# An attention and two dense layers on one core: decays as repeated rows, the causal mask by short products, guards in pairs

## The chip, the cores and the metric

The kernel runs on one core of a Trainium2 chip. Its time is that of one execution on the device in microseconds (us); the runs' median is what two versions are compared by. The engines are called as the profile calls them: PE (matrix products), PEld (its weight loads), DVE (vector), ACT (scalar), POOL (GpSimd) and SP, which issues DMAs; PEq, SPq and so on are an engine's instruction queue.

## The reference

Attention with a decay per head, then a mixture of four experts, then a gated layer. Only the attention is touched by the change:

```python
B, H, S, D = q.shape                      # 2, 8, 576, 64
scores = (1 / np.sqrt(D)) * np.matmul(q, k.transpose(0, 1, 3, 2))
cum = np.cumsum(np.maximum(s, 0.0), axis=-1)
bias = -(cum[:, :, :, None] - cum[:, :, None, :])
scores = np.where(causal, -1e9, scores + np.minimum(bias, 0.0))
attn = np.exp(scores - scores.max(-1, keepdims=True))
attn = attn / (attn.sum(-1, keepdims=True) + 1e-09)
out = np.matmul(attn, v)
...
x = moe(out); return gated(x)             # x: 1152 x 512
```

## The kernel before

Sixteen heads (two batches of eight) are worked two at a time. A *pair* is two heads whose 64 rows of Q and K stand in the two halves of the partitions. The sequence of 576 is cut into blocks of 128 rows (the last has 64). The program first takes the *early* blocks 0 and 1 of all pairs (pairs 0 to 7), then the *late* blocks 2, 3 and 4 (pairs 8 to 15, which are the same heads again). Block 4 has 64 rows, so both heads of a pair share one tile of 128 rows there; this is the two-head block.

For each pair the function `scores` multiplies Q and K in float32 into PSUM (`sp`) and adds the decay on PE: `rk` and `lq` hold the running sums of `s` in two fp32r halves and ones, so that a second product over 64 rows, or 128 for the two-head block, adds cum[key] - cum[query]. The sums are made in `scan` on 16 partitions, split in two halves in `cums` and brought to the rows of `rk` and `rq` by eight DMAs (`rows_of`); `sel` picks a pair's rows when `lq` is scaled. The constant term of a row falls out when the row's minimum is taken off. Then `chain` does, for each head and block of rows: `least` (DVE: adds the causal `mask`, scales, writes `ns` and takes the row's minimum), `exp` (ACT), `guard` (DVE: adds 1e-9 and takes the reciprocal), `norm` (division by the sum, on DVE or POOL), `turn` (PE transposes the blocks of `ns` into `tp`), `copy` (ACT or DVE, into `p`). `products` multiplies by V into `po`, and `values` writes the result in two halves, `xh` and `xl`.

The dense layers read `xh` and `xl`. Weights come by DMA into `raw` and are split into two fp32r halves (`wah` and `wal`, `woh` and `wol`), in the attention stage on POOL. The first dense unit needs the early blocks of four pairs only, so dense products (h and o) stand between the pieces of attention. All instructions are put in order ahead of the run by a planner (`Plan`): every task names its engine or several, its cost, what it depends on, buffers that it takes and gives back, and a rank; the planner starts the earliest task that can go, and where PE would be idle ahead of the first dense output it puts in transposes of the identity (`keep_on`, L426). Engines and DMA queues then work strictly in that order. PSUM holds two score banks `sp`, two `tp`, one `po`, and the dense `h` and `o`.

Of the kernel before, what the change touches and what calls it, by code (L numbers as in the profile page):

```python
# [17 lines left out]
P = 128  # L18
# [8 lines left out]
NL = 3  # L27
# [15 lines left out]
NORM = "pv"  # L43
# [46 lines left out]
def f32(ap):  # L90
    return ap.bitcast(F32)
# [177 lines left out]
def attention_moe_swiglu(ctx, tc, q_early, q_late, k, v, s, dp, w1, w2, wg, wv, wo, out):  # L269
# [23 lines left out]
    wp = ctx.enter_context(tc.tile_pool(name="wp", bufs=2))  # L293
    psw = ctx.enter_context(tc.tile_pool(name="psw", bufs=1, space=PSUM))
# [43 lines left out]
    def attention(ap, ps):  # L338
        one = ap.tile([P, S], F32, name="one", tag="ns", bufs=NS)[:B * H, :]
        sr = ap.tile([P, NB - 1, 320], F32, name="sr", tag="p", bufs=NPT).rearrange("p c t -> p (c t)")[:B * H, :S]  # L340
        ncum = ap.tile([P, S], F32, name="ncum", bufs=1)[:B * H]
        cums = ap.tile([LO + B * H, S], F32R, name="cums", bufs=1)
        cum_at = [slice(0, B * H), slice(LO, LO + B * H)]
# [3 lines left out]
        rk = ap.tile([P, S], F32R, name="rk", bufs=1)  # L347
        rq = ap.tile([P, S], F32, name="rq", bufs=1)
        sel = ap.tile([P, 3, BP], F32, name="sel", bufs=1)

        mask = ap.tile([P, BANK + P], F32, name="mask", bufs=1)
        mask2 = ap.tile([P, D], F32, name="mask2", bufs=1)


        t_sr = add("dma", (0.48, 0.1), lambda: nc.sync.dma_start(sr, s), take=[ring("p", NPT)], rank=-100)
        t_one = any_of("vp", "fill", S - 2 * P, lambda e: {"v": nc.vector, "p": nc.gpsimd}[e].memset(
            one[:, :S - 2 * P], 1.0), [], take=[ring("ns", NS)], rank=-99)
        t_id = add("pool", 0.6, lambda: make_identity(nc, ident), rank=-99)

        def upper():  # L360
            nc.gpsimd.memset(mask[:, BANK:], 0.0)
            nc.gpsimd.affine_select(
                out=mask[:, BANK:], in_=mask[:, BANK:], pattern=[[-1, P]], compare_op=ALU.is_ge, fill=-8.0e30, base=0,
                channel_multiplier=1)
        t_up = add("pool", 0.6, upper, [t_id], rank=-92)
        t_zero = []
        for o, r in ((slice(BANK - P, BANK), -91), (slice(0, BANK - P), 10)):
            t_zero.append(any_of("vp", "fill", o.stop - o.start, lambda e, o=o: {
                "v": nc.vector, "p": nc.gpsimd}[e].memset(mask[:, o], 0.0), [], rank=r))

        def twice(e):
            for x in half:
                move(e, mask2[x, :], mask[x, BANK + x.start:BANK + x.stop])
        t_mask = [t_up, t_zero[0]]
        t_mask2 = [t_up, *t_zero, any_of("vp", "copy", P, twice, [t_up, t_zero[1]], n=2, rank=12)]
# [9 lines left out]
        def rows_of(x, at, deps, rank):  # L385

            t = at
            for i, e in enumerate("vv" if not x.start else "vp"):
                def part(on, i=i):
                    if i:  # L390
                        minus(on, cums[cum_at[1], x], ncum[:, x], cums[cum_at[0], x])
                    else:
                        move(on, cums[cum_at[0], x], ncum[:, x])
                t = any_of(e, "two" if i else "copy", x.stop - x.start, part, [t], rank=rank)
                for j, (to, of) in enumerate(((rk, 2 * i), (rq, 2 * i + 1))):
                    got = fetch(lambda to=to, of=of: f32(to[of::8, x]), f32(cums[cum_at[i], x]), 16, [t] + deps, rank + 0.1 + 0.1 * j)
                    t_rows[x.start].append(got)

        def fetch(to, x, kb, deps, rank, take=(), queue=None):

            return add("dma", (ISSUE, kb * DMA_KB), lambda: (queue or nc.sync).dma_start(to(), x), deps, take=take, rank=rank)

        early, later = slice(0, 2 * P), slice(2 * P, S)
        t_rows = {0: [], 2 * P: []}
        t_fill = [any_of("vp", "fill", 2 * P, lambda e, x=x, y=y: {"v": nc.vector, "p": nc.gpsimd}[e].memset(f32(x[:, early]), y), [], rank=-97)
                  for x, y in ((rk, -1.0), (rq, 1.0))]
# [4 lines left out]
        def pick():  # L411
            nc.vector.reduce_sum(sel[:, 1:].rearrange("p h m -> p (h m)"), ident.rearrange("p (m r) -> p m r", r=8)[:, :, :4], axis=AX.X)
            nc.vector.tensor_tensor(sel[:, 0], sel[:, 1], sel[:, 2], op=ALU.add)
        t_pick = add("dve", 0.35, pick, [t_id], rank=-96)
        t_fill2 = [any_of("p", "fill", S - 2 * P, lambda e, x=x, y=y: nc.gpsimd.memset(f32(x[:, later]), y), [], rank=CUM2)
                   for x, y in ((rk, -1.0), (rq, 1.0))]
        t = any_of("p", "fill", S - 2 * P, lambda e: positive(e, later), [t_sr], rank=CUM2)
        t_scan2 = add("dve", dve(S - 2 * P), lambda: scan(later), [t, t_scan], give=[(t_sr, ring("p")), (t_one, ring("ns"))], rank=CUM2)
        rows_of(later, t_scan2, t_fill2, CUM2)
# [26 lines left out]
        t_ready, t_scores, qs, lq = {}, {}, {}, {}  # L446

        def prepare(pi, release):
# [9 lines left out]
            def to():  # L458
# [5 lines left out]
            parts = [(0, x.start, 0, 2 * P)] if exact else [(0, x.start, 0, 2 * P)] + [  # L464
                (1 + j, 4 * P, 2 * P + j * D, 2 * P + j * D + D) for j in range(2)]
            done = []
            for kind, a, o, e in parts:
                def pick(on, kind=kind, a=a, o=o, e=e):
                    if pi not in lq:
                        lq[pi] = ap.tile([P, n], F32R, name="l" + tag, tag="l" + tag, bufs=NL)  # L470
                    scale(on, lq[pi][:, o:e], rq[:, a:a + e - o], sel[:, kind, m:m + 1])
                done.append(any_of(SPLIT, "scale", e - o, pick, [release, t_pick] + t_rows[x.start][1::2] + done[:1],
                                   take=[] if done else [ring("l" + tag, NL)], rank=rank + 0.2))
            t_ready[pi] = [tk, tq] + done + t_rows[x.start][::2]
            used[pi] = [(tq, ring(tag)), (done[0], ring("l" + tag))]
# [10 lines left out]
        def scores(i, pi, qbs, last):  # L486

            m = pi % BP
            two = rows(qbs[0]) < P
            w = [qb * P + rows(qb) for qb in qbs]  # L490
            box = {"sp": {}}

            def run():
                Q, K, L = qs[pi], keys[m], lq[pi]
                if two:
                    for s0, s1 in ((0, BANK), (BANK, w[0])):
                        sp = ps.tile([P, BANK], F32, name="sp", tag="sp", bufs=2)
                        nc.tensor.matmul(sp[:, :s1 - s0], Q[:, 2 * P:], K[:, s0:s1], start=True, stop=False)  # L498
                        nc.tensor.matmul(sp[:, :s1 - s0], L[:, 2 * P:], rk[:, s0:s1], start=False, stop=True)
                        box["sp"].setdefault((None, qbs[0]), []).append(sp)  # L500
                    return
                sp = [ps.tile([P, BANK], F32, name="sp", tag="sp", bufs=2) for j in range(2)]
                at = 0
                for qb, n in zip(qbs, w):
# [4 lines left out]
                    for j in range(2):  # L509
                        box["sp"][j, qb] = [sp[j][:, at:at + n]]  # L510
                    at += n
            cost = sum(pe32(n) + pe(n) for n in w) + SWITCH
            t = inorder("s", add("pe", cost, run, t_ready[pi] + [before.get("s")], take=[ring("sp")] * 2,
                                 give=used[pi] if last else [], rank=i + RANK["s"]))
            return t, box["sp"]

        def chain(i, pi, ch, j, qb, tS, banks, last_of):

            g = pi // NP
            n = rows(qb)  # L520
            w = qb * P + n
            heads = [j] if j is not None else [0, 1]
            two = len(heads) == 2
            row = {h: slice(x * n, (x + 1) * n) for x, h in enumerate(heads)}
            spans = [(a, min(w, a + BANK)) for a in range(0, w, BANK)]
            box = {}

            def least():
                st = box["st"] = ap.tile([P, 6], F32, name="st", tag="st", bufs=8)
                box["ns"] = ap.tile([P, S], F32, name="ns", tag="ns", bufs=NS)  # L530
                for x, ((s0, s1), sp) in enumerate(zip(spans, banks[j, qb])):
# [1021 lines left out]
```

## Time and profile before

| | |
|---|---|
| median of 3 runs | 721.79 us (721.7 to 722.0) |
| profiled execution: own time, span | 723.54 us, 721.8 us |
| PE busy | 705.4 us, 98% of the span |
| DVE, ACT, POOL busy | 563.6, 350.6, 481.6 us |
| mean granted clock of PE | 0.991 |
| moved by DMA | 71.74 MB, 99 GB/s over the span |

The span runs from the first to the last instruction. PE's busy time is the union of its records, whose ends are modelled, so the distance between starts tells more on the rate of products than their length. A float32 product is two records in the trace and one row in the order of the program; a transpose is one.

### The profile page before, as it was taken

The page shows a single profiled execution, that of the slowest core. Times are in us where ns is not written, and L with a number is a line of the kernel's source. Part 1 is how long each engine was busy: PE and PEld are TensorE (multiplying, and loading weights), DVE is VectorE, ACT ScalarE, POOL GpSimd, SP SyncE. Part 2 cuts the span into 40 slices and gives each one's busy share as a digit, 9 for nine tenths or more (in the row PEclk, how much of TensorE's full clock was granted, in tenths as well). Part 3 has the DMA queues.
Part 4 walks back from the last instruction along what each step waited for, and adds up shares of the span by engine and source line. Part 5 has one row for each costly group of instructions (what it writes and reads, how often), then busy time and mean ns, then how long its engine had stood idle before and what let it go on. Part 6 is the DMA issues. An engine that isn't in the chain of part 4 may idle for free.

```text
span 721.8 us, 11989 instructions
## 1 busy us (share of the span) xinstructions
PE 705.4 (98%) x4256; PEld 609.1 (84%) x4256; DVE 563.6 (78%) x1146; ACT 350.6 (49%) x776; POOL 481.6 (67%) x460
## 2 busy tenths in 40 slices
PE   7899999999999999999999999999999999999997
PEld 6576666688898888898989899998889999999996
DVE  4787767598278799999999897577876878787665
ACT  3687665443434555565565554375654324233210
POOL 3664544699456578765777577699899768585321
PEclk7899999999999999999999999999999999999999
DMA  5362341011304454573455544102011202000003
GB/s 154 136 201 95 115 136 41 30 31 58 117 1 146 163 159 162 178 228 132 147 177 203 190 139 140 58 31 88 30 59 59 63 31 84 30 30 1 1 1 131
DMA packets 26554, 71.74 MB, mean 99 GB/s; under 512 B 3184, under 2 KB 7408, under 8 KB 26496
## 3 DMA queue, kind: packets, MB, share of 16 engines
q1 hardware_dynamic: 26352, 70.86, 29.6%
q8 instruction: 33, 0.54, 0.3%
q14 instruction: 25, 0.20, 0.1%
q10 hardware_dynamic: 144, 0.13, 0.1%
HBM read 59.04 MB, written 11.80 MB: 98 GB/s over the span
## 4 chain that ended last, share of the span: by engine, by line
PE 84%; DVE 9%; issue 2%; POOL 2%; ACT 1%; DMA 1%; SPq 0%; DVEq 0%; POOLq 0%; ACTq 0%
PE o L1120 11%; PE o L1121 11%; PE o L1122 11%; PE h L1058 11%; PE h L1060 11%; PE h L1059 11%; PE sp L508 4%; PE tp L567 3%; PE po L616 3%; PE h L958 2%; PE h L960 2%; PE h L959 2%; DVE tt L997 2%; DVE cc L1077 1%; PE sp L498 1%
## 5 line engine op out<-in xcount | busy, mean ns | idle before, releaser
L1077 DVE TENSOR_TENSOR cc<-cc,h 128x320 f32<-128x320 f32 (+1 forms) x282 | 125.2, 452 | 48.8 <-PE h L1060 43.4
L1120 PE MATMUL o<-woh,hh 128*128 128x512 f32 x396 | 157.6, 398 | 1.6 <-DVE acc_b L1208 0.9
L1121 PE MATMUL o<-wol,hh 128*128 128x512 f32 x396 | 155.9, 394 | 0.0
L1122 PE MATMUL o<-woh,hl 128*128 128x512 f32 x396 | 154.9, 391 | 0.1
L1058 PE MATMUL h<-xh,wsh 128*128 128x320 f32 (+1 forms) x312 | 93.0, 298 | 0.0
L1060 PE MATMUL h<-xh,wsl 128*128 128x320 f32 (+1 forms) x312 | 92.9, 298 | 0.0
L1059 PE MATMUL h<-xl,wsh 128*128 128x320 f32 (+1 forms) x312 | 92.8, 297 | 0.0
L327 POOL TENSOR_TENSOR wal<-raw,wah 128x512 fp32r<-128x512 f32 (+1 forms) x58 | 74.3, 1290 | 27.5 <-ACT wah L314 26.5
L1122 PEld LDWEIGHTS o<-woh,hl 128*128 128x128 f32 x396 | 74.5, 188 | 17.1 <-POOL hl L327 0.6
L1120 PEld LDWEIGHTS o<-woh,hh 128*128 128x128 f32 x396 | 74.6, 188 | 16.0 <-DVE acc_b L1208 1.6
L327 POOL TENSOR_TENSOR hl<-cc,hh 128x512 fp32r<-128x512 f32 (+1 forms) x29 | 43.5, 1500 | 64.8 <-ACT hh L1180 61.5
L327 POOL TENSOR_TENSOR wol<-raw,woh 128x512 fp32r<-128x512 f32 x54 | 78.7, 1470 | 9.4 <-ACT woh L314 8.9
L1121 PEld LDWEIGHTS o<-wol,hh 128*128 128x128 f32 x396 | 74.6, 188 | 10.6
L1177 ACT ACTIVATE cc<-cc 128x640 f32<-128x640 f32 (+1 forms) x46 | 32.0, 696 | 80.8 <-DVE cc L1077 80.8
L1058 PE MATMUL h<-xh,wah 128*128 128x320 f32 (+1 forms) x234 | 69.5, 297 | 0.7 <-DVE cc L1077 0.7
L1060 PE MATMUL h<-xh,wal 128*128 128x320 f32 (+1 forms) x234 | 69.4, 297 | 0.0
L1059 PE MATMUL h<-xl,wah 128*128 128x320 f32 (+1 forms) x234 | 69.4, 296 | 0.0
L327 POOL TENSOR_TENSOR wsl<-sf,wsh 128x512 fp32r<-128x512 f32 x44 | 65.4, 1505 | 0.5 <-ACT wsh L314 0.4
L324 POOL TENSOR_SCALAR ns<-ns,st 128x512 f32<-128x512 f32 (+4 forms) x39 | 22.8, 586 | 60.1 <-DVE st L546 42.9
L1208 DVE SCALAR_TENSOR_TENSOR acc_b<-o,pr,acc_b 128x512 f32<-128x512 f32 x75 | 55.6, 743 | 8.0 <-PE o L1122 7.6
L1058 PEld LDWEIGHTS h<-xh,wsh 128*128 128x128 f32 x312 | 59.0, 189 | 1.5
L1059 PEld LDWEIGHTS h<-xl,wsh 128*128 128x128 f32 x312 | 59.0, 189 | 1.4
(150 smaller groups left out, 1748.8 us busy)
## 6 DMA issues: line engine op xcount, KB each, us to landing
raw<-in_w SPq DMA_DIRECT2D x42, 512.0 KB, 4.5
n<-hl SPq DMA_DIRECT2D x36, 256.0 KB, 2.4
raw<-n SPq DMA_DIRECT2D x18, 512.0 KB, 3.3
hh<-in_wg SPq DMA_DIRECT2D x12, 512.0 KB, 3.8
hh<-in_wv SPq DMA_DIRECT2D x12, 512.0 KB, 4.5
hh<-in_wo SPq DMA_DIRECT2D x12, 512.0 KB, 4.2
vr<-in_v SPq DMA_DIRECT2D x4, 640.0 KB, 4.0
ql<-in_q_late SPq DMA_DIRECT2D x8, 192.0 KB, 3.1
```

What stands on the lines that cost most here:

```text
L324: {"v": nc.vector, "p": nc.gpsimd}[e].tensor_scalar(to, x, by, 1.0, op0=ALU.mult, op1=ALU.mult)
L327: {"v": nc.vector, "p": nc.gpsimd}[e].tensor_tensor(to, x, f32(y), op=ALU.subtract)
L508: nc.tensor.matmul(sp[j][:, at:at + n], y[half[j], x], z[half[j], :n], start=first, stop=not first)
L1058: nc.tensor.matmul(hp, wh, h, start=c == 0, stop=False)
L1059: nc.tensor.matmul(hp, wh, l, start=False, stop=False)
L1060: nc.tensor.matmul(hp, wl, h, start=False, stop=c == 1)
L1077: nc.vector.tensor_tensor(part(k), part(x), banks[i], op=ALU.add)
L1120: nc.tensor.matmul(op, hh[:, f, ts], wh[:, f, :], start=f == 0, stop=False)
L1121: nc.tensor.matmul(op, hh[:, f, ts], wl[:, f, :], start=False, stop=False)
L1122: nc.tensor.matmul(op, hl[:, f, ts], wh[:, f, :], start=False, stop=f == NF - 1)
L1177: nc.scalar.activation(src()[:, o], src()[:, o], AF.Relu)
L1208: nc.vector.scalar_tensor_tensor(acc(t), bank_(), sc, acc(t), op0=ALU.mult, op1=ALU.add)
```

## The change

- The decays are no longer added on PE. `sums` holds the running sum with one column taken off (`center`); it is written to memory, and for each pair a DMA repeats a head's row over the partitions (`dqe` for early pairs, `dql` and, for the two-head block, `d2`). `least` adds these where it added the mask. For pairs 0 and 1 (`NSEL`) PE selects the row by a product with a column of the identity instead, and ACT copies it.
- The causal mask is added on PE: `idr` (identity, 64 rows at a time) times `tri` (0 and -2^103), 128 and 64 columns for each head and block. In the two-head block the mask is added to `d2`'s last 64 columns.
- `scores` and `chain` become `group`. One `guard` serves two rows of sums; the transposes of both early blocks of a head go into one bank and one copy; early score banks of pairs 1 and 3 come from the dense `h` banks.
- `norm` runs on POOL alone (`NORM = "p"`).

```diff
-NL = 3
+NBE = 3
+NBL = 2
+NSEL = 2
...
-NORM = "pv"
+NORM = "p"
...
+        def center(x, at):
+            nc.vector.tensor_scalar(sums[:, x], ncum[:, x], ncum[:, at:at + 1], 1.0, op0=ALU.subtract, op1=ALU.mult)
...
-        rows_of(early, t_scan, t_fill, -97.5)
+        t_early = add("dve", dve(2 * P), lambda: center(early, P - 1), [t_scan], rank=-98)
+        t_rows = [fetch(lambda: rows_e, sums[:, early], 16, [t_early], -97.5)]
...
-                    scale(on, lq[pi][:, o:e], rq[:, a:a + e - o], sel[:, kind, m:m + 1])
...
+            if pi < NSEL:
+                def pick():
+                    bias()
+                    tp = ps.tile([P, BANK], F32, name="tp", tag="tp", bufs=2)
+                    for j in range(2):
+                        nc.tensor.matmul(tp[:, j * w:j * w + w], ident[:BH, BP * j + m:BP * j + m + 1].to_broadcast([BH, P]),
+                                         sums[:, early], start=True, stop=True)
...
+            else:
+                of = rows_e if exact else rows_l
+                first = fetch(bias, lambda: of[m::BP, :w].partition_broadcast(P), 2 * w // 2, [release, t_rows[-1]], rank + 0.2, take=[rg])
...
+                    t2.append(fetch(both(j), lambda j=j: rows_l[BP * j + m, :].partition_broadcast(D), 144, [release, t_rows[-1]] + t2,
+                                    rank + 0.3, take=[] if j else [ring("d2", NBL)]))
...
-                    for y, z, first in ((Q, K, True), (L, rk, False)):
+                    for j in range(2):
+                        nc.tensor.matmul(sp[j][:, at:at + w], Q[half[j], x], K[half[j], :w], start=True, stop=False)
+                    for o, y in enumerate((slice(0, P), slice(P, P + D))):
                         for j in range(2):
-                            nc.tensor.matmul(sp[j][:, at:at + n], y[half[j], x], z[half[j], :n], start=first, stop=not first)
+                            nc.tensor.matmul(sp[j][:, at + w - P + o * D:at + w], idr[half[j], o, :], tri[half[j], y], start=False, stop=o == 1)
...
-                nc.vector.tensor_scalar(st[:, 4:5], st[:, 2:3], 1.0e-9, None, op0=ALU.add)
-                nc.vector.reciprocal(st[:, 5:6], st[:, 4:5])
+                    nc.vector.tensor_scalar(st[:, 12 + x:12 + x + n], st[:, 8 + x:8 + x + n], 1.0e-9, None, op0=ALU.add)
+                    nc.vector.reciprocal(st[:, 16 + x:16 + x + n], st[:, 12 + x:12 + x + n])
```

The planner puts everything in a new order. First PE, from the start of the program to the scores of the first pair (k_104 and the like are a pair's keys, o<-ident the transposes that keep PE moving). Before:

```order
L426 MATMUL o<-ident 128x128 x29
L508 MATMUL sp<-k_104,qe 128x128 x2
L508 MATMUL sp<-rk,lqe 128x128 x2
L508 MATMUL sp<-k_104,qe 128x256 x2
L508 MATMUL sp<-rk,lqe 128x256 x2
L426 MATMUL o<-ident 128x128 x3
```

and after:

```order
L399 MATMUL o<-ident 128x128 x14
L451 MATMUL tp<-sums,ident 128x256 x4
L516 MATMUL sp<-k_106,qe 128x128 x2
L519 MATMUL sp<-tri,idr 128x128 x2
L519 MATMUL sp<-tri,idr 128x64 x2
L516 MATMUL sp<-k_106,qe 128x256 x2
L519 MATMUL sp<-tri,idr 128x128 x2
L519 MATMUL sp<-tri,idr 128x64 x2
L516 MATMUL h<-k_107,qe 128x128 x2
```

The selections of two pairs stand ahead of the first scores, each block's rk products have become four short mask products, and the second pair's scores follow the first's at once, in h banks. Ahead of the first dense product PE has 7 score groups, 34 transposes and 6 value groups before; after, 4 selections, 7 score groups, 30 transposes and 4 value groups. There are 58 transposes of the identity before and 44 after, 10 of them behind the first dense product.

On POOL the place is the early pairs (ns<-ns,st is a division; wah, wal, woh, wol are weights). Before:

```order
L324 TENSOR_SCALAR ns<-ns,st 128x128
L318 TENSOR_SCALAR wah<-raw 128x512
L327 TENSOR_TENSOR wal<-raw,wah 128x512
L324 TENSOR_SCALAR ns<-ns,st 128x256
L318 TENSOR_SCALAR wah<-raw 128x512
L318 TENSOR_SCALAR woh<-raw 128x512
L327 TENSOR_TENSOR wal<-raw,wah 128x512
L327 TENSOR_TENSOR wol<-raw,woh 128x512
```

and after, a little further on:

```order
L327 TENSOR_SCALAR ns<-ns,st 128x128
L327 TENSOR_SCALAR ns<-ns,st 128x256
L321 TENSOR_SCALAR wah<-raw 128x512
L327 TENSOR_SCALAR ns<-ns,st 128x128
L327 TENSOR_SCALAR ns<-ns,st 128x256
L330 TENSOR_TENSOR wal<-raw,wah 128x512
L327 TENSOR_SCALAR ns<-ns,st 128x128
L327 TENSOR_SCALAR ns<-ns,st 128x256
```

Pieces of weights now stand singly between the divisions of each head. On SP, behind the first loads of Q and K, the two pairs of transfers from cums have become one write of the sums and one repeated read. Before:

```order
L401 DMA rk<-cums 16x256 x2
L401 DMA rq<-cums 16x256 x2
L401 DMA k_107<-in_k 128x256
L401 DMA qe<-in_q_early 128x256
L401 DMA vr<-in_v 128x512 x2
```

and after:

```order
L358 DMA rows_104<-sums 16x256
L358 DMA dqe<-rows_104 128x2x256
L358 DMA k_109<-in_k 128x256
L358 DMA qe<-in_q_early 128x256
L358 DMA vr<-in_v 128x512 x2
L358 DMA rows_105<-sums 16x576
```

The keys of the fourth pair and the loads after them stand behind the repeated read of pair 2, as they stood behind the reads of cums.

## Rows read from the trace of the kernel before

**Rows 1.** Stretches: busy us (x records) by engine, PEclk, DMA share, GB/s.

```profile
core 0: us, PE busy (x) PEld busy (x) DVE busy (x) ACT busy (x) POOL busy (x), PEclk, DMA share, GB/s
12.50:42.10 29.60, 25.77 (x174) 18.26 (x175) 23.85 (x122) 20.68 (x83) 18.06 (x24) 0.82 0.47 157
42.10:60.00 17.90, 17.84 (x140) 13.53 (x139) 14.56 (x68) 15.01 (x54) 9.51 (x15) 1.00 0.66 213
60.00:140.00 80.00, 79.73 (x499) 51.87 (x497) 56.18 (x193) 50.79 (x141) 38.09 (x49) 1.00 0.23 77
```

**Rows 2.** Groups by line and shape on PE, 12.5 to 42.1 us.

```profile
L567 PE MATMUL tp<-ident,ns 128*128 128x128 f32 x33 | 7.7, 321 | 3.6 <-ACT p L314 2.1 <-DVE ns L324 1.3
L426 PE MATMUL o<-ident 128*128 128x128 f32 x29 | 5.8, 320 | 0.0
```

**Rows 3.** Order of time at the start: start us, us, engine, line, [idle before <-releaser].

```profile
3.46 0.82 DVE L381 TENSOR_TENSOR_SCAN ncum<-one,sr 16x256 f32<-16x256 f32 x1
...
6.41 1.22 SPq L401 DMA_DIRECT2D rq<-cums  x2
...
7.22 0.49 PE L508 MATMUL sp<-k,qe 64*128 64x128 f32 x4
...
8.94 1.28 ACT L322 ACT_TABLE_LOAD   x1 [8.94 <-DMA rq<-cums]
...
10.79 0.47 PE L508 MATMUL sp<-rk,lqe 64*128 64x128 f32 x2 [3.08 <-ACT lqe L322]
```

**Rows 4.** Order of time on PE: one early pair.

```profile
35.80 0.49 PE L508 MATMUL sp<-k,qe 64*128 64x128 f32 x4
...
36.88 0.87 PE L616 MATMUL po<-p,vr 128*64 128x256 f32 x8
37.68 0.55 PE L567 MATMUL tp<-ident,ns 128*128 128x128 f32 x3
38.06 0.71 PE L426 MATMUL o<-ident 128*128 128x128 f32 x5
```

**Rows 5.** Order of time on PE: two late score groups, and dense products.

```profile
76.66 1.02 PE L498 MATMUL sp<-k,ql 128*128 128x512 f32 x2
77.12 0.80 PE L499 MATMUL sp<-rk,lql 128*128 128x512 f32 x1
77.75 0.33 PE L498 MATMUL sp<-k,ql 128*128 128x64 f32 x2
77.89 0.28 PE L499 MATMUL sp<-rk,lql 128*128 128x64 f32 x1
78.00 1.09 PE L567 MATMUL tp<-ident,ns 128*128 128x128 f32 x8
...
85.96 1.13 PE L508 MATMUL sp<-k,ql 64*128 64x512 f32 x4
...
87.25 0.87 PE L567 MATMUL tp<-ident,ns 128*128 128x128 f32 x6
...
147.06 0.39 PE L1120 MATMUL o<-woh,hh 128*128 128x512 f32 x1
147.29 0.40 PE L1121 MATMUL o<-wol,hh 128*128 128x512 f32 x1
```

**Rows 6.** Groups on DVE, then on POOL, 12.5 to 42.1 us.

```profile
L324 DVE TENSOR_SCALAR ns<-ns,st 128x256 f32<-128x256 f32 x9 | 5.3, 591 | 0.2
...
L324 DVE TENSOR_SCALAR ns<-ns,st 128x128 f32<-128x128 f32 x7 | 3.7, 527 | 0.1
...
L327 POOL TENSOR_TENSOR wal<-raw,wah 128x512 fp32r<-128x512 f32 x4 | 5.2, 1295 | 0.1
...
L324 POOL TENSOR_SCALAR ns<-ns,st 128x256 f32<-128x256 f32 x3 | 1.4, 476 | 1.2 <-ACT xh L314 1.2
```

**Rows 7.** A group on ACT, 0 to 165 us.

```profile
L314 ACT COPY p<-tp 128x512 f32<-128x512 f32 x10 | 5.9, 586 | 10.2 <-PE tp L567 10.2
```

**Rows 8.** DMA issues: KB each, median us to landing.

```profile
raw<-in_w SPq DMA_DIRECT2D x42, 512.0 KB, 4.5
...
rq<-cums SPq DMA_DIRECT2D x2, 16.0 KB, 1.8
```

More of the change, by code (lines that the diff above doesn't have):

```diff
@@ L345, in attention @@
+        sr = ap.tile([P, NB - 1, 320], F32, name="sr", tag="p", bufs=NPT).rearrange("p c t -> p (c t)")[:BH, :S]
+        ncum = ap.tile([P, S], F32, name="ncum", bufs=1)[:BH]
+        sums = ap.tile([P, S], F32, name="sums", bufs=1)[:BH]
+        early, later, whole = slice(0, 2 * P), slice(2 * P, S), slice(0, S)
+        rows_e, rows_l = (scratch.tile([BH, n], F32, name=f"rows{n}", bufs=1) for n in (2 * P, S))
         QW = 3 * P
         keys = [ap.tile([P, S], F32, name=f"k{i}", bufs=1) for i in range(BP)]
-        rk = ap.tile([P, S], F32R, name="rk", bufs=1)
@@ L348, in attention @@
[L348 to L357, printed above, removed]
+        mask = ap.tile([P, P], F32, name="mask", bufs=1)
@@ L358, in attention @@
         t_id = add("pool", 0.6, lambda: make_identity(nc, ident), rank=-99)
         def upper():
-            nc.gpsimd.memset(mask[:, BANK:], 0.0)
+            nc.gpsimd.memset(mask, 0.0)
             nc.gpsimd.affine_select(
[L363 to L375, printed above, removed]
+                out=mask, in_=mask, pattern=[[-1, P]], compare_op=ALU.is_ge, fill=-2.0 ** 103, base=0, channel_multiplier=1)
+        t_up = add("pool", 0.6, upper, [t_id], rank=-98)
+        lo, hi = half
+        t_clear = [any_of("v", "fill", 2 * P, lambda e: nc.vector.memset(f32(idr).rearrange("p o n -> p (o n)"), 0.0), [], rank=-97),
+                   any_of("v", "fill", D, lambda e: nc.vector.memset(f32(tri[hi, hi]), -2.0 ** 103), [], rank=-97)]
@@ L383, in scan @@
                 op0=ALU.mult, op1=ALU.add)
[L385 to L397, printed above, removed]
@@ L474, in prepare, with bias @@
-            t_ready[pi] = [tk, tq] + done + t_rows[x.start][::2]
-            used[pi] = [(tq, ring(tag)), (done[0], ring("l" + tag))]
+            if not exact and pi == EXACT:
+                t_mid = add("dve", dve(S), lambda: center(whole, 3 * P + P // 4 - 1), [t_scan2, t_early] + t_rows, rank=CUM2)
+                t_rows.append(fetch(lambda: rows_l, sums, 36, [t_mid], CUM2))
+            w = 2 * P if exact else BANK
+            def bias():
+                decay[pi] = ap.tile([P, 2, w], F32, name="d" + tag, tag="d" + tag, bufs=NBE if exact else NBL)
+                return decay[pi]
@@ new lines, in norm, with run @@
+            def norm(x, lane, at, w):
+                def run(on):
+                    ns = box["ns"][lane][:, at:at + w]
+                    scale(on, ns, ns, box["st"][:, 16 + x:17 + x])
+                return run
+            ready, bias = t_ready[pi]
+            cost = sum(pe32(w) for _, _, w in segs) + (0.1 if two else 0.13 * len(segs) + SWITCH)
+            tS = inorder("s", add("pe", cost, scores, ready + [before.get("s")], take=[rg] * 2, rank=i + RANK["s"]))
+            exps, owner = [], {}
@@ new lines, in group @@
+            todo = [(x, lane, seg) for x, (lane, seg) in enumerate((l, s_) for l in range(len(lanes)) for s_ in segs)]
+            for x, lane, (qb, at, w) in todo:
+                new, final = lane not in owner, x == L - 1
+                tM = inorder("m", add("dve", dve(w, len(spans)) + 0.01, least(x, lane, at, w), [tS, before.get("m")] + bias,
+                                      take=[ring("ns", NS)] if new else [], give=[(tS, rg)] + (used[pi] if qbs[-1] == ch.qbs[-1] else [])
+                                      if final else [], rank=i + x + RANK["m"]))
+                owner.setdefault(lane, tM)
+                exps.append(inorder("e", add("act", act(w) + 0.23, exp(x, lane, at, w), [tM, before.get("e")], rank=i + x + RANK["e"])))
```

268 lines of the change are left out of this document (139 added, 129 removed).

## The prediction

> **What bounds the kernel now.** I read the table of stretches first [rows 1], then, stretch by stretch, PE's groups and the order of time. From 42.1 us on the matmul engine (PE) is never short of work: 17.84 of 17.90 us, then 79.73 of 80.00. A microsecond of PE work that goes there is a microsecond of the kernel, and nothing that ACT, DVE or POOL save there counts as long as they keep up (60 to 140: DVE 56, ACT 51, POOL 38 of 80). Ahead of 42.1 it is otherwise. The first score product that holds the decays runs at 10.79, and between 12.5 and 42.1 PE's busy 25.77 us are swollen: 29 of its 174 records are transposes of the identity that only keep it moving [rows 2], and the granted clock is 0.82.
>
> How much is lost there? Dense work begins at 42.1, the start of L958's first product. One early pair of heads costs PE 1.08 us of scores (35.80 to 36.88), 0.80 of values (to 37.68) and 0.127 a transpose (three, 37.68 to 38.06) [rows 4]. Ahead of the first dense product the program has 7 score groups, 34 transposes and 6 value groups: 7.6 + 4.3 + 4.8 = 16.7 us. So 42.1 - 16.7 = **25.4 us** of PE are lost at the start. That number and the sum of PE work make up the kernel's time; the change is costed in both.
>
> **The start.** Before: the scan starts at 3.46 and lasts 0.82; then come two halves of the sums, two pairs of DMAs on SP's queue (the second pair issued from 6.41), a table load that waited for them until 8.94, an operand scaled by head, and the product at 10.79 [rows 3]. After: scan, on DVE one centring and casts for the mask between them, which I estimate at 0.7 together, less than the scan's own 0.82: 5.0; then four float32 products select the heads' rows. PE runs them at what price? The trace has no such product. A float32 product of 512 columns and its fp32r one take 1.09 together (76.66 to 77.75), and 0.23 is the distance of dense fp32r products of 512 [rows 5]; the rest, 0.86, makes 0.43 for 256 columns, 1.7 for four. Scores of pair 0 then start at 6.7. K and Q are there by then (at 7.22 PE waited for nothing shown [rows 3]); ACT's copy of 512 columns, 0.59 [rows 7], lies beside the second two selections, and its table load has no wait now. That is 4 us earlier than 10.79.
>
> **The pace of early pairs.** Six pairs pass in 12.5 to 42.1 (of the seven score groups the first is over by then): 4.9 us each. Of the three other engines DVE is busiest, 23.85 us or 4.0 a pair [rows 1]. Its 16 divisions take 9.0 of that [rows 6] and go to POOL; half the guards go too. That leaves at most 14.9, or 2.5 a pair. POOL gets 16 divisions of at most 0.48 (7.6); in its new order only 4 of the 8 remainders of weights stand ahead of the same point, which gives back 5.2 [rows 6]: 20.5 / 6 = 3.4 a pair, with all copies of weights still counted. ACT's 20.68 are 3.4 a pair, without counting that its operand scalings go. PE: rows of rk cost 0.18 a pair by the dense distance (0.06 + 0.12) and leave; mask products come, two pieces per block row and head, the two heads in the two halves of the array. That halves run side by side shows in 85.96 to 87.25: two heads took 1.29 where one over the full array took 1.09 [rows 5]. The nearest row to a mask piece is the 64-column fp32r product, 0.11 (77.89 to 78.00); two pieces are 0.22 a block row, bounds 0.09 (by columns alone) and 0.44 (each head by itself). So scores are 1.08 - 0.18 + 0.44 = 1.34, and PE needs 1.34 + 0.76 + 0.80 = 2.9 a pair. Slowest are ACT and POOL, 3.4; I take 3.5. Bounds: 2.9, where ACT's scalings and half of POOL's copies are gone and PE's sum is left, and 4.9 as now.
>
> Seven score groups then end at 6.7 + 6 x 3.5 + 1.3 = 29.0. I add 1.5 for late DMAs: the repeated rows of pairs 2 to 7, 256 KB each, join a queue that already moves 157 GB/s [rows 1], behind 512 KB weights that took 4.5 us to land [rows 8]. Dense work starts at **30.5** (bounds 25.4 and 37.4). By the new order PE has then done 7 x 1.34 + 30 x 0.127 + 4 x 0.80 + 1.7 = 18.1 us of use. Lost: 30.5 - 18.1 = 12.4, which is **13.0 less** than 25.4 (bounds 18.1 and 6.1 less).
>
> **PE work of the whole program.** The selections add 1.7, the early pairs 8 x 0.26 = 2.1 (bounds 0 and 5.6). In the eight late pairs rk goes: 0.17 (384 columns) + 0.23 (512) + 0.34 (the two-head block, 512 and 64) = 0.74; two mask groups of 0.22 come: 0.30 less a pair, **2.4** in all (bounds 4.5 less and 1.1 more). Transposes, values and dense columns keep their numbers: six early stages of 256 columns and four of 512 become four and five, as many columns. Sum: +1.4. Idle transposes: ten of the 44 now stand behind the start of dense work, +1.3.
>
> It matters how rk is priced. Read by starts, the 512-column rk product holds the next one off for 0.63 us (77.12 to 77.75), the same shape in the dense part for 0.23 [rows 5]. I take 0.23: PE works down float32 records whose second half still runs when the fp32r record begins. The Trainium skill, page "FP8 and Floating Point Precision", section "TensorE Precision Notes", says that true FP32 takes four passes through the array; four and one at 0.23 would be 1.15, and the trace's 1.09 agrees, whereas 0.63 for one pass does not. By the rule the sum is the one above; by the start distances it is that of rival 1.
>
> **What moves and hides.** A division of 256 columns takes 0.48 on POOL and 0.59 on DVE by the means [rows 6], so the move itself is costed at nothing; but on POOL it can stand behind a remainder of 1.3. Behind 42 us dense products cover that, and POOL, 38 of 80 us busy [rows 1], has room. In the early pairs, where the cover is thin, it is what the step from 2.9 to 3.5 a pair pays for. SP's queue has the wait for the rows' way through memory (two transfers, 1.8 each by the nearest row [rows 8]) ahead of k3 and the later Q, where it now has two waits for cums; pairs 0 and 1 don't need it. In late pairs three transfers (512 KB and twice 144 KB) wait for the last minimum of the pair two before, and SP queues weights behind them. They have about a pair's time: from the two-head group of one pair at 76.66 to the 512-column group of the next at 85.96 it is 9.3 [rows 5], about 11 by estimate to its two-head group. By the raw row's 114 GB/s [rows 8] they take 7.
>
> **Sum**: -13.0 + 1.4 + 1.3 = -10.3. The profiled span is 721.8 and its execution took 723.5, 1.7 around it; the runs' median is 721.8. I take the change from the median: **711.5 us**.
>
> **Rivals.**
> 1. *rk cost its start distances*, 0.63 for 512 columns and by columns 0.47, 0.32 and 0.16 for 384, 256 and 128. Then a late pair loses 0.47 + 0.63 + 0.63 + 0.11 = 1.84 and gets 0.44: 1.4 less, 11.2 over eight instead of 2.4; early pairs lose 0.48 and get 0.44, 0.3 less in all instead of 2.1 more. For it: the distances stand in every late pair. Against: the 1.09. The sum would be 11.2 lower: 700.
> 2. *The pace stays.* Another chain (scores, minimum, exponential, division, transpose, copy, values, remainder), not DVE's sum, sets 4.9 us a pair; from pair 4 on scores still have one pair of banks. For it: DVE is 81% busy, not full, and PE waited 2.1 us for ACT's copies and 1.3 for DVE's divisions [rows 2]. Then dense work starts at 37.4: -6.1 + 1.4 + 1.3 = -3.4: 718.4.
> 3. *Repeated rows come late: slower.* A late pair needs 800 KB that it did not need. It decides where they take longer than a pair's 11 us, or about 70 GB/s. Should reading one row 128 times halve the raw row's rate, they take 14 us, 3 late: 24 us over eight pairs against the gain of 10.3: 735. From 1.3 us a pair on the kernel gets slower. For it: 213 GB/s flow already in 42 to 60. Against: the share of the DMA engines is 0.66 there and 0.23 in 60 to 140.
> 4. *Nothing moves*: POOL's queue, with weights between its divisions, holds the weights back as much as the start gives: 722.
>
> **Chances.** Forecast 0.62, rival 1 0.10, rival 2 0.13, rival 3 0.10, rival 4 0.05. Range: the forecast's own bounds reach from 702 to above 720; with rival 2 inside and rivals 1 and 3 outside I give 703 to 719.5. A measurement of this kernel tells about 0.2% from no change. Faster 0.85 (forecast and rivals 1 and 2), same 0.04, slower 0.11.
>
> **What would show it.** The first scores with masks at about 6.7 and the first L981 product at 28 to 33; early scores 3.5 us apart; the late 512-column score group about as long as its 1.29 before, not 0.7; the two-head group at 1.0 instead of 1.34; PE full behind the start; no minimum waiting for dql or d2. I am wrong if PE's idle time behind 31 us grows by more than some 3 us, with a DMA or POOL named ahead of it, or if the early pairs still come 4.9 apart.

## The result: slower by 1.1%

The changed kernel takes **730.78 us** (four runs, 727.63 to 731.33) beside 721.89 of the kernel before on the same chip: ratio **1.0109**, 95% interval 1.0076 to 1.0141. The forecast was 711.5, its range 703 to 719.5. A second comparison, on another chip and with twelve runs, gave 727.84 beside 723.16, ratio 1.0069 (1.0049 to 1.0090). So the change costs 5 to 9 us. Ratios are taken over undisturbed executions; the quotient of two medians can differ from them in the third decimal.

The profiled execution is the fastest of the first four: 727.63, span 725.8, 4.1 longer than the span before. Its stretches, which answer to [rows 1], with one more from behind the attention:

```profile
core 0: us, PE busy (x) PEld busy (x) DVE busy (x) ACT busy (x) POOL busy (x), PEclk, DMA share, GB/s
12.50:42.10 29.60, 26.39 (x222) 21.01 (x218) 17.18 (x94) 20.07 (x74) 17.84 (x34) 0.88 0.87 244
42.10:60.00 17.90, 15.80 (x104) 11.93 (x106) 8.63 (x30) 9.04 (x26) 16.60 (x24) 0.90 0.79 252
60.00:140.00 80.00, 78.30 (x493) 52.76 (x490) 47.80 (x153) 45.08 (x123) 40.51 (x57) 1.00 0.42 125
160.00:180.00 20.00, 17.74 (x94) 15.15 (x93) 19.97 (x28) 5.72 (x14) 16.58 (x16) 1.00 0.27 79
```

The kernel before in the last of these stretches:

```profile
160.00:180.00 20.00, 19.51 (x102) 16.85 (x101) 17.91 (x25) 8.06 (x18) 19.08 (x19) 1.00 0.22 71
```

PE, full from 42.1 on before, now idles 2.1 us in 42 to 60, 1.7 in 60 to 140 and 2.3 in 160 to 180. The DMA engines move 244 GB/s in the early stretch where they moved 157. The start, in order of time, answers to [rows 3]:

```profile
start us, us, engine line op out<-in xcount [idle before <-releaser]
...
3.14 0.92 DVE L381 TENSOR_TENSOR_SCAN ncum<-one,sr 16x256 f32<-16x256 f32 x1
...
4.83 1.99 PE L451 MATMUL tp<-sums,ident 16*128 16x256 f32 x8
...
6.75 0.49 PE L516 MATMUL sp<-k,qe 64*128 64x128 f32 x4
...
33.76 0.39 PE L981 MATMUL h<-xh,wah 128*128 128x256 f32 x1
```

Four selections take 1.92 us (4.83 to 6.75), scores begin at 6.75 instead of 10.79, and the first dense product comes at 33.76 instead of 42.13. That lead of 8.4 us is gone by the end. Between 6.75 and 32.53 the seven early score groups start 4.30 us apart, where the forecast had 3.5. This start is not that of every execution: in the second profile, of the same kernel, the selections take 3.71 and scores begin at 8.54 (see the last section).

Two groups of a late pair answer to [rows 5]:

```profile
59.00 1.13 PE L516 MATMUL sp<-k,ql 64*128 64x512 f32 x4
59.56 0.71 PE L519 MATMUL sp<-tri,idr 64*128 64x128 f32 x4
60.20 0.50 PE L1143 MATMUL o<-woh,hh 128*128 128x512 f32 x1
...
77.03 1.19 PE L511 MATMUL sp<-k,ql 128*128 128x512 f32 x4
78.06 0.39 PE L587 MATMUL tp<-ident,ns 128*128 128x128 f32 x2
```

The 512-column group holds PE 1.20 us (1.29 before), the two-head group 1.03 (1.34 before). So PE's work did not grow. What it waits for (engine, tile and line, who releases it; us in all, times, longest):

```profile
PE tp L587 <- POOL ns L327: 3.5, 2, 2.0
PE o L1143 <- DVE acc_a L1231: 3.0, 3, 1.6
PE h L516 <- DVE st L533: 2.6, 1, 2.6
PE h L1081 <- DVE cc L1100: 2.1, 2, 1.4
```

Behind the first of these stands POOL's queue, here in order of time from 37 us, and then what PE does meanwhile:

```profile
37.20 1.62 POOL L327 TENSOR_SCALAR ns<-ns,st 128x128 f32<-128x128 f32 x4
42.18 0.32 POOL L476 TENSOR_TENSOR d<-d,tri 128x64 f32<-128x64 f32 x1 [3.35 <-DMA d<-rows]
42.47 0.61 POOL L321 TENSOR_SCALAR wah<-raw 128x512 fp32r<-128x512 f32 x1
43.05 0.61 POOL L321 TENSOR_SCALAR woh<-raw 128x512 fp32r<-128x512 f32 x1
43.65 0.83 POOL L327 TENSOR_SCALAR ns<-ns,st 128x128 f32<-128x128 f32 x2
...
44.08 0.90 PE L587 MATMUL tp<-ident,ns 128*128 128x128 f32 x3 [2.00 <-POOL ns L327]
...
47.05 1.70 PE L399 MATMUL o<-ident 128*128 128x128 f32 x7
```

The addition of the mask to `d2`'s last 64 columns (L476, 0.32 us long) waits 3.35 us for its rows. It serves a late pair's two-head block, whose scores come at 53.16, but POOL works in the order of its queue: two weights and two divisions of an early pair stand behind it, and PE's transposes stand behind those; seven transposes of the identity at 47.05 fill PE's time and do no work. Five of the eight late pairs' additions stand on POOL, three on DVE; POOL waits for rows at all five, DVE at two, and once a minimum (`least`, L533) waits on DVE for a late pair's rows. The first three lines are these waits (us in all, times, longest); the others are times from issue to landing, which answer to [rows 8]:

```profile
POOL d L476 <- DMA d<-rows: 13.6, 5, 4.5
...
DVE d L476 <- DMA d<-rows: 4.3, 2, 2.7
DVE ns L533 <- DMA d<-rows: 3.6, 1, 3.6
...
raw<-in_w SPq DMA_DIRECT2D x42, 512.0 KB, 5.1
...
dql<-rows SPq DMA_DIRECT2D x8, 512.0 KB, 5.6
...
d<-rows SPq DMA_DIRECT2D x16, 144.0 KB, 5.9
dqe<-rows SPq DMA_DIRECT2D x6, 256.0 KB, 6.7
...
qe<-in_q_early SPq DMA_DIRECT2D x7, 128.0 KB, 6.1
```

**Time at equal work.** Columns of the dense products, added up in order of start, say how far the dense layers have come. When the 70,000th starts, the attention is over in every kernel here; the 1,200,000th starts some 49 to 50 us ahead of the end in all. This gives three marks for each profile (us; in brackets against the kernel before; the last column is what is lost between the second and third mark):

| kernel | first dense | 70,000th column | 1,200,000th | lost behind |
|---|---|---|---|---|
| before | 42.13 | 147.99 | 672.40 | 0 |
| changed | 33.76 | 147.15 (-0.8) | 676.52 (+4.1) | 4.95 |
| changed, second profile | 35.80 | 147.18 (-0.8) | 676.34 (+3.9) | 4.75 |

So there are two losses: one inside the attention, which eats nearly all of the lead won at its start, and one of 5 us behind it, where nothing was meant to change.

### The profile page after: what moved, and what is told of

The parts are those of the page before. It is cut to its first block, busy times and chain, and to the rows that moved or that the text cites. A ratio compares the mean times of both kernels' runs of the same rounds, so it can differ in the third digit from the quotient of the medians.

```text
span 725.8 us, 11966 instructions
## 1 busy us (share of the span) xinstructions
PE 706.1 (97%) x4274; PEld 611.9 (84%) x4274; DVE 554.3 (76%) x1063; ACT 340.4 (47%) x729; POOL 484.4 (67%) x482
## 4 chain that ended last, share of the span: by engine, by line
PE 73%; DVE 11%; DMA 6%; issue 4%; ACT 2%; POOL 2%; SPq 1%; DVEq 0%; POOLq 0%; ACTq 0%
PE o L1143 10%; PE o L1145 10%; PE o L1144 10%; PE h L1081 10%; PE h L1083 10%; PE h L1082 10%; PE po L646 3%; DVE tt L1020 3%; PE tp L587 2%; PE sp L516 2%; DMA dqe<-rows 2%; DMA d<-rows 2%; PE h L981 1%; DVE acc_a L1231 1%; DVE cc L1100 1%
## 5 line engine op out<-in xcount | busy, mean ns | idle before, releaser
L330 POOL TENSOR_TENSOR wal<-raw,wah 128x512 fp32r<-128x512 f32 (+1 forms) x58 | 70.6, 1225 | 39.5 <-ACT wah L317 36.2
L330 POOL TENSOR_TENSOR hl<-cc,hh 128x512 fp32r<-128x512 f32 (+1 forms) x24 | 37.2, 1553 | 49.6 <-ACT hh L1203 48.9
L327 POOL TENSOR_SCALAR ns<-ns,st 128x128 f32<-128x128 f32 (+3 forms) x72 | 39.2, 556 | 42.5 <-DVE st L549 34.3
```

The lines of the kernel that those rows point to most:

```text
L327: {"v": nc.vector, "p": nc.gpsimd}[e].tensor_scalar(to, x, by, 1.0, op0=ALU.mult, op1=ALU.mult)
L330: {"v": nc.vector, "p": nc.gpsimd}[e].tensor_tensor(to, x, f32(y), op=ALU.subtract)
```

## The experiments

Three theories. **A:** the repeated rows come late, and what waits for them holds up others: minima on DVE, the additions (most of them on POOL) and the divisions and weights behind them. **B:** divisions on POOL alone are the wait, rows or no rows. **C:** the loss behind the attention is one of the plan's order and of its dealing (which engine it gives each piece of work), not of the work.

**Rows loaded once.** All other instructions stay, in the same order; pairs behind the first take its rows and load none of their own.

```diff
 def bias():
+    if pi > (NSEL if exact else EXACT):
+        decay[pi] = decay[NSEL if exact else EXACT]
+        return None
```

(The same in `both`, for `d2`.)

> The changed kernel, with the repeated rows loaded once: the rows of pair 2 serve all later early pairs and those of pair 8 all later late pairs, so the decays of the other pairs are wrong; 12 pairs' transfers, 6.9 MB, and the waits for them are gone, and every other instruction stands where it stood. Theory A (the rows load the DMA queues and land late; minima, the tail addition on POOL and what stands behind both wait): the about 7.5 us that the changed kernel loses between its first dense product (33.8) and the last attention values (141) mostly come back, PE is not idle around 42 to 50 and 65, and the time is 722 to 725, 0.8 to 1.2% under the changed kernel's 730.8. Theory B (divisions on POOL alone are the wait): the transfers cost nothing to speak of and the time stays at 729 to 731. Theory C (the new order as such loses the time, behind 141 too): 729 to 731 as well.

Measured: 721.52 beside 722.96, ratio 0.9987 (0.9972 to 1.0003). A's number. First dense product 31.93, early scores 3.99 us apart, 70,000th column at 140.78 (-7.2), lost behind 5.85. The rows cost 6.4 us inside the attention by these marks; C stays as a second loss.

**No addition of the mask**, neither the five on POOL nor the three on DVE.

```diff
 def tail(on):
-    {"v": nc.vector, "p": nc.gpsimd}[on].tensor_tensor(y, y, f32(tri[:, P:]), op=ALU.add)
+    return
```

> The changed kernel without the addition of the mask to the last 64 columns of the two-head block's rows (the causal mask of that block is left out), every other instruction where it stood. POOL, which runs its queue in order, then never waits for these transfers. If the rows' lateness hurts by this queue (POOL waited 13.6, 5 and 4.5 us for them, with divisions and weights behind it), 3 to 4 us come back: 727. If the minima's own wait is what hurts, less than 1: 730.

Measured: 724.57 beside 722.96, ratio 1.0014 (0.9998 to 1.0030); 70,000th at 144.55 (-3.4), lost behind 4.15. One addition per late pair, 0.3 us each, was worth 0.55 to 0.95% in all, more than expected. PE's wait for divisions (3.5 us before the edit) is nearly gone although all rows are still loaded:

```profile
PE tp L587 <- POOL ns L327: 0.3, 1, 0.3
```

**Divisions on DVE or POOL.**

```diff
-NORM = "p"
+NORM = "pv"
```

> The changed kernel with divisions allowed on DVE again beside POOL, as before. Theory B (a division stands in POOL's queue behind remainders of weights and behind the tail addition, and PE's transposes wait for it): the 3.5 us that PE waits for POOL's divisions go, 725 to 727. Theory A: the same transfers come as late and are waited for elsewhere, 729 to 732.

Measured: 726.41, ratio 1.0053 (1.0040 to 1.0066). By number this is B's. But 70,000 columns came at 148.79 (+0.8), no earlier than in the changed kernel (the profiled execution took 728.26, near the slowest of its six), and PE still waits 4.3 us for POOL's divisions and 2.2 for DVE's. So what made it faster is not shown; whether POOL alone is bad without the block is asked further down.

**Early rows all selected by PE** (`NSEL = 8` for 2).

> The changed kernel with the early pairs' rows all picked out by PE from the sums, as pairs 0 and 1 have them: six transfers of 256 KB less in the first 30 us, 12 more selections and their copies on PE and ACT. By the first selections' price of some 0.43 us PE gets 5.2 us more work. Theory A: the wait for the early rows (2.6 us at 17) and what the queue passes on from there go, about 4 to 6 us: 729 to 732. If the early rows cost nothing: 736.

Measured: 739.83 (729.73 to 742.49), ratio 1.0195 (1.0151 to 1.0240). A miss for both expectations. In its profile PE was granted 0.50 from 12 to 36 us while busy all that time, and the first dense product came at 48.46. But that is not the whole: an execution with a mean granted clock of 1.000 took 739.35. So this run settles nothing on the early rows.

**The changed kernel again**, for a second profile.

> The changed kernel once more, unedited, as the neighbour of the three runs beside it and for a second profile: 1.011 times the kernel before, 728 to 732. If its granted clock at the start differs from the first profile's 0.85 (12.5 to 35), the first dense product moves with it.

The result stands above. Its first scores came 1.8 and its first dense product 2.0 later than in the first profile, and its 70,000th column at the same time.

**Six early stages of 256 columns.** This was meant to give the early stages of the kernel before, and does not. In the traces the product of `xh` and `wah` (L958, after the change L981) has eight records for an early stage of 256 columns, and eight more from some 390 us on for the other half of its rows. So the kernel before has three such stages and four of 512, the changed kernel two and five, and this run six and two; the prediction's six and four stages of 256 columns counted both halves.

```diff
-t1 = EARLY if len(done_x[1]) < NP or any(x.end is None for x in done_x[1]) else HALF
+t1 = EARLY if i < 6 else HALF
```

> The changed kernel with the early dense stages made as before: six of 256 columns, then four of 512, instead of four and five (the same columns in all). Theory C (behind the attention the changed kernel loses about 5 us, because the other division into stages puts one whole stage more behind it, in which PE waits for DVE's accumulators at 164, 178, 263, 287): most of the 5 us come back, 725 to 727, and PE's waits for acc behind 140 fall to about 1.3 us. If the division has no part in it: 729 to 732.

Measured: 739.97 beside 723.16, ratio 1.0226 (1.0203 to 1.0249). A miss: at 70,000 columns it is where the changed kernel is (147.21), and then it loses 15.2 us instead of 5, and at the end another 0.7 for 1,536 columns more, at 0.45 ns each by the dense distance in [rows 5]. What the earlier division is worth by itself, this run doesn't tell. Others speak against it as the cause: the run with divisions on DVE or POOL came out with three and four, as the kernel before, and loses 3.95; a run further down loses 0.12 with two and five.

**The two-head mask by PE.** One product with a whole identity replaces the addition on POOL.

```diff
+nc.tensor.matmul(sp[1][:, :D], idw, tri[:, P:], start=False, stop=True)
...
-tb.append(any_of("vp", "two", D, tail, t2 + t_mask, rank=rank + 1))
+tb += t2
```

> The changed kernel, with the mask of the two-head block's last 64 columns added by one product on PE (a whole identity in float32r against the 64-column triangle) instead of the addition on POOL; no instruction of POOL waits for the repeated rows any more, and the output stays the reference's. Theory A by POOL's queue: the gain of the run without the addition, less eight products of some 0.1 us: 724 to 726, ratio to before 1.003. If what helped there was the smaller work and not the wait: 729 to 731.

Measured: 719.00 beside 723.16, ratio **0.9949** (0.9932 to 0.9965): faster than both kernels. All rows are still loaded, as slowly (`d` 5.9, `dql` 5.8, `dqe` 6.5 us), but nothing on POOL waits for them. 70,000th at 144.26 (-3.7). The plan came out otherwise this time, with three early stages of 256 columns and 49,664 dense columns inside the attention instead of 61,952, and the loss behind it is 0.44. So this run changes more than the addition; the run without the addition is the clean test.

**Both of these edits.**

> The two edits together, six and four early stages and the mask by PE. If theory A (POOL's queue) and theory C (the stages) are two separate losses, they add: 719 to 722, at or under the kernel before. If one edit takes what the other would have given: 724 to 726.

Measured: 738.47, ratio 1.0201 (1.0178 to 1.0224); 70,000th at 144.03 (-4.0), lost behind 18.9. A miss: with six and two stages the loss is large again; the mask's gain inside the attention stays.

**The kernel before with divisions on POOL alone** (`NORM = "p"`).

> The kernel before with divisions on POOL alone, the one part of the change that can be made by itself. Theory B (POOL's queue of divisions and weights is a wait by itself, without any repeated rows in it): slower by 2 to 4 us, 725 to 727, with PE waiting for POOL's divisions. Theory A (only the wait for transfers that stands in that queue makes it late): within 1 us of before, 722 to 724.

Measured: 726.11 beside 723.62, ratio 1.0034 (1.0022 to 1.0046), B's number once more. Yet its profile is 1.5 ahead at the 70,000th column and PE waits only 0.47 and 0.26 for POOL's divisions; it loses 1.7 behind the attention, and its plan has 1,536 columns more, 0.7 us by the price above.

**Mask by PE, divisions on POOL or DVE.**

> The kernel with the two-head mask on PE and divisions on POOL or DVE. Now no transfer stands in POOL's queue. Theory A: the divisions' place no longer matters and the time is that of its neighbour with the mask on PE, 0.995 of before, 719 to 720 (within 1.5 us). Theory B: the divisions on POOL alone still cost, and this is 2 us faster or more: 717.

Measured: 722.21, ratio 0.9984 (0.9971 to 0.9997), 0.35% slower than with POOL alone. With no wait for rows in POOL's queue, the attention ends no later with divisions on POOL alone: 144.26 against 145.06 here, 146.47 against 147.99 in the kernel before, one profile each. So B is not supported inside the attention. The differences of the whole times, 0.35%, are of the size that the dealing alone makes (below), and say nothing on the divisions.

**Another dealing behind the attention.** `HELD2` is the handicap for DVE when the plan chooses an engine for work behind the attention; up to 146 us DVE, ACT and POOL do the same instructions in the same order.

> The changed kernel with one number changed that the plan uses only behind the attention: the handicap it gives to DVE when it chooses between engines, 0.5 for 1.0. Up to 141 us everything stays. If the 4 to 6 us lost behind the attention come from how that work is dealt to engines (C, the order), the loss changes by some us in either direction, mostly up here, since DVE, full from 160 to 180, gets more: 729 to 735. If the loss is one that any order has: unchanged, 728 to 730.

Measured at 0.5: 734.60, ratio 1.0156 (1.0143 to 1.0169), lost behind 10.6.

> The same with 2.0 for 1.0: DVE gets less behind the attention. C, the order: PE's waits for acc_a at 164 and 178 shrink, 1 to 4 us less: 724 to 727. Any order has it: 728 to 730.

Measured at 2.0: 740.06, ratio 1.0220 (1.0196 to 1.0244), lost behind 18.4, the wrong way for the expectation. PE's waits for DVE at 164 and 178 went as expected, and POOL fell behind instead. PE in order of time at 519 us:

```profile
519.40 0.28 PE L1082 MATMUL h<-xl,wsh 128*128 128x256 f32 x1
527.68 0.58 PE L1083 MATMUL h<-xh,wsl 128*128 128x256 f32 x1 [8.00 <-POOL wsl L330]
```

Then both kernels with a tenth either way; PE's order is the same as with 1.0 in all but the third.

> The changed kernel with the plan's handicap for DVE behind the attention at 0.9 for 1.0; PE's order is the same, some DVE, ACT and POOL work is dealt otherwise. C, the dealing: the loss between 144 and 677 us at equal dense columns, 5 us now, changes by 2 us or more in either direction. The work itself: 4 to 6 us again.

Measured: 723.08 beside 723.37, ratio 0.9996 (0.9984 to 1.0008). Lost behind: **0.12** instead of 4.95, in the profile of its slowest execution (726.34). PE's waits there:

```profile
PE o L1143 <- DVE acc_a L1231: 2.3, 2, 1.6
...
PE h L1081 <- ACT cc L317: 1.0, 1, 1.0
...
PE o L1145 <- DVE hl L330: 0.5, 1, 0.5
PE h L1081 <- DVE cc L1100: 0.4, 2, 0.2
```

> The same at 1.1 for 1.0. C, the dealing: a loss other than 5 us by 2 us or more, in either direction. The work itself: 4 to 6 us again.

Measured: 726.95 (722.86 to 733.05), ratio 1.0052 (1.0030 to 1.0073); lost behind 1.58 in its profile, which is its fastest run.

> The kernel before at 0.9 for 1.0. C, the dealing: it is as sensitive as the changed kernel and, being moved off the order it has, loses 1 to 5 us, 724 to 728. The work itself: within 1 us of before.

Measured: 725.51, ratio 1.0033 (1.0018 to 1.0047), lost behind 2.1.

> The kernel before at 1.1 for 1.0, PE's order the same. C, the dealing: a loss of 1 to 5 us, 724 to 728. The work itself: within 1 us of before.

Measured: 721.05, ratio 0.9970 (0.9959 to 0.9981): 1.7 *won* behind. C holds: the same work, PE's order unchanged, and 5 us come and go with which engine does it. The kernel before was not at its best either.

**Mask by PE, rows loaded once.**

> The kernel with the two-head mask on PE, the repeated rows loaded once (pair 2's for all later early pairs, pair 8's for all later late pairs; the other pairs' decays are wrong), order unchanged. If late rows cost only by POOL's queue: within 1 us of its neighbour, 0.995 of before, 719 to 720. If minima still wait for them and transfers behind them come late: 2 to 4 us less, 715 to 717.

Measured: 715.15 beside 723.50, ratio 0.9889 (0.9874 to 0.9904). First dense product at **30.69**, 70,000th at 138.28 (**-9.7**), lost behind 1.19. So the rows still cost 0.6%, 4.3 us, where POOL doesn't wait for them. With them, the run with the mask by PE has two waits that are gone here, of minima for early pairs' rows and of POOL for weights:

```profile
DVE ns L536 <- DMA dqe<-rows: 4.5, 2, 3.9
...
POOL wah L321 <- DMA raw<-in_w: 4.4, 2, 2.6
```

Which of the two costs how much, no run tells.

**Mask by PE, handicap 1.1.**

> The kernel with the two-head mask on PE and the plan's handicap for DVE behind the attention at 1.1 for 1.0, PE's order unchanged. The dealing at 1.1 was 1.7 us better than 1.0 in the kernel before and 3.4 in the changed one; with the mask on PE the loss behind the attention is only 0.3 us at 1.0, so from a gain of 2 us (717) to a loss of 2 us (721).

Measured: 718.37, ratio **0.9933** (0.9920 to 0.9947): no different from 1.0 within the intervals. These two are the versions to keep. Against the kernel before at 1.1 (0.9970) they are ahead by 0.2 and 0.4% only.

## Why the prediction was wrong

**The start: the order right, two terms too small.** Scores came at 6.75 (forecast 6.7) and the selections took 1.92 (1.7) in the first profile, but that is luck of the execution: in 11 of the 15 profiles in which PE selects the rows of two pairs they took 3.7, and scores came at 8.54 to 8.58. The pace, "I take 3.5", measured 4.30, and 3.99 and 3.49 in the two runs without the rows. The first dense product was put at 30.5 with 1.5 in it for late DMAs, so at 29.0 without them. Without the rows it comes at 30.69 and 31.93; with them, in six profiles of the changed kernel's early order, at 33.3 to 36.8. The step "I add 1.5 for late DMAs" was mis-sized: against 31.93, the same order without the rows, they cost 1.4 to 4.9.

**PE's work: right.** The two late groups came out at 1.20 and 1.03; the forecast's terms make 1.28 and 1.00. Rival 1 would have taken some 0.4 off the 512-column group; it is refuted. The Trainium skill's four passes for true FP32 (page "FP8 and Floating Point Precision", section "TensorE Precision Notes") led to the right one of the two prices here.

**The step that failed: "What moves and hides".** It gave the late pairs' three transfers a pair's time and asked only whether a *minimum* would wait. It did not cost the addition of the mask to `d2` at all, though five of the eight stand on POOL with divisions behind them, and it read that POOL, 38 of 80 us busy [rows 1], "has room". Room in time didn't help where the engine worked in order and stood still: POOL waited 13.6 us for these rows. (A minimum waited as well, once, for 3.6 us.) Taking away the additions and their wait alone gave 0.55 to 0.95%, all of the rows 0.8 to 1.2%. The prediction's own sign of being wrong came true: from 42 to 140 us PE idled 3.8 us, 0.3 before, and the longest of its waits was for POOL. Rival 3 named the cause, late rows, and put it at the wrong place and size: 24 us in all, by halved transfers; measured 6.4 with the early rows, at most 0.8 a late pair, which is under its own point of decision, 1.3. That its number, 735, was the nearest is luck: the dealing added 5 us to what the rows cost. Its halved rate was not seen: `dql` lands 512 KB in 5.6 us, weights of that size in 5.1.

**The term that was missing.** The sum ended with the attention and took for granted that the rest keeps its distance. Instead the plan, run anew, dealt that rest otherwise, and it cost 4.95 us more. No line of the diff touches that work.

The account, by the marks of the profiles:

| | us |
|---|---|
| forecast at the end of attention and of the kernel | -10.3 |
| measured without late rows: mask by PE / changed order | -9.7 / -7.2 |
| rows come late, 2.6 of it by the additions' wait | +6.4 |
| changed kernel at the end of attention | -0.8 |
| dealing behind the attention | +5.0 |
| changed kernel, span against span | +4.1 |

The medians say 5 to 9 rather than 4; the first profile is the fastest run of its four. What stays open: these marks are of one execution each, and six profiles with the changed kernel's early order scatter from 145.75 to 149.76 at the 70,000th column (three of the kernel before: 147.18 to 147.99), so the +6.4 is good to some 2 us; the ratios carry it. By the ratios the additions' wait is two thirds or more of what the rows cost, by the marks 2.6 of 6.4, and with the mask by PE the rows still cost 0.6%: how the loss divides is not settled. And I have not shown which single decision of the plan makes the 5 us, only that dealing decides. Rival 2 is out: the pace did change, though by less than forecast. Rival 4 (722) was partly right in cause, POOL's queue, but what held the queue was a transfer, not the weights.

## What to carry to other kernels

For each new wait, ask on which engine's in-order queue it stands and what is queued behind it; an engine that is half idle can still be what everyone waits for, here one instruction of 0.2 to 0.3 us per pair that waited for a transfer cost 0.55 to 0.95%. Where a planner lays out the whole program, a change in one stage re-deals all later stages: compare times at equal work behind the change before crediting or blaming the change itself, and re-tune the plan's numbers for each version. For this kernel a forecast needs a term of some 5 us for the dealing alone: the versions of the changed kernel that differ in the handicap alone lost 0.1 to 18.4 us behind the attention.

## What the runs showed of the hardware

The granted clock of the first 50 us differs between executions that begin alike. Two kernels in stretches of 4 us, first the one with all early rows selected by PE, then the one with the mask by PE:

```profile
core 0: us, PE busy (x) PEld busy (x) DVE busy (x) ACT busy (x) POOL busy (x), PEclk, DMA share, GB/s
...
4.00:8.00 4.00, 3.27 (x14) 2.31 (x13) 2.50 (x7) 1.17 (x2) 0.46 (x1) 1.00 0.67 189
8.00:12.00 4.00, 4.00 (x30) 3.43 (x29) 0.65 (x5) 0.90 (x3) 0.00 (x0) 0.60 0.93 262
12.00:16.00 4.00, 4.00 (x17) 2.70 (x15) 3.11 (x20) 2.60 (x11) 2.36 (x6) 0.50 1.02 383
...
32.00:36.00 4.00, 4.00 (x23) 3.11 (x22) 0.34 (x2) 1.47 (x5) 2.40 (x4) 0.50 0.24 63
```

```profile
8.00:12.00 4.00, 4.00 (x28) 3.29 (x28) 1.48 (x8) 1.23 (x4) 0.00 (x0) 1.00 0.50 145
...
24.00:28.00 4.00, 1.86 (x11) 1.09 (x11) 1.53 (x10) 1.41 (x6) 2.21 (x6) 1.00 0.84 260
```

The first fell to the lower level (0.50, 1.2 GHz) after PE had idled 0.69 us for a copy in 4 to 8, and stayed there to 36 us with PE's records covering all of the time, in a program of selections, scores and transposes. In that stretch being busy did not bring the clock back. The second is at the upper level (2.4 GHz) in 24 to 28, through 2.1 us of idle time. The first profile of the changed kernel has a stretch at 0.50 too, from 20 to 24.

The clock column is not the whole story at the start. In the second kernel it says 1.00 from 8 to 12 us, yet PE's products there take about twice as long as the same products in the first profile of the changed kernel (shown at the start: 1.99 for the selections, 0.49 for the first scores):

```profile
4.83 3.77 PE L453 MATMUL tp<-sums,ident 16*128 16x256 f32 x8
8.54 0.80 PE L519 MATMUL sp<-k,qe 64*128 64x128 f32 x4
...
13.95 0.49 PE L519 MATMUL sp<-k,qe 64*128 64x128 f32 x4
```

From 13.95 on they are back at 0.49. In the run with all early rows selected by PE the same scores take 0.80 at 16.11, where the column says 0.50. So products at the pace of the lower level can stand under a 1.00 at the start of a profile; go by the distance of equal products. Eleven of the 15 profiles counted above start so. It moves the first scores by 1.8 us, and may be part of the scatter of the first dense product; no run tells how much.

A row read from memory and repeated over 128 partitions lands about as fast as a weight of that size (5.6 and 5.1 us for 512 KB); while the repeated rows were under way the core moved up to 398 GB/s (20 to 24 us of the first profile of the changed kernel).
